# Queueing the low-word step of a float64 weight slice on ScalarE directly behind the high-word step

## The chip, the cores and the metric

The kernel runs on one core of one Trainium2 chip. The metric is the device time of one execution in microseconds (us), taken as the median of several executions. Engines are named as in the profile: PE is TensorE's matmul, PEld its weight load, DVE is VectorE, ACT is ScalarE, POOL is GpSimd, SP is SyncE, which here issues nearly all transfers. "L204" is line 204 of the kernel before; lines of the changed kernel from 210 on stand one higher.

## The reference

The reference has two parts. The first is a recurrent retention layer over 4 batches, 8 heads, 768 positions and head size 64. The second takes its output as 3072 rows of 512 numbers through a two-layer block with SiLU between:

```python
for t in range(S):
    state = gamma[None, :, None, None] * state + np.einsum('bhd,bhe->bhde', k[:, :, t], v[:, :, t])
    y[:, :, t] = scale * np.einsum('bhd,bhde->bhe', q[:, :, t], state)
...
x = np.ascontiguousarray(attn_out.transpose(0, 2, 1, 3)).reshape(B * S, H * D)
...
h = x @ w_in
g = h * (1.0 / (1.0 + np.exp(-h)))
return (g @ w_out).astype(np.float32)
```

q, k and v are float32. The weights `w_in` (512 by 2048) and `w_out` (2048 by 512) come as float64, because they are float32 arrays multiplied by a float64 scalar. The kernel turns them into float32 on the chip.

## The kernel before

**Tiles.** The sequence is cut into 6 chunks of 128 positions; a chunk and a batch make one of 24 units. The retention layer is done by chunks: transposes of k and q, scores within the chunk, a state carried between chunks, and the output y. A "visit" is the work of one step of this pipeline on PE. The first product multiplies, for each chunk c (512 columns, 4 batches) and each of 16 slices f of `w_in` (128 columns), x by the weights. It takes 12 matmuls: x and w are each split in a high and a low part, 8 matmuls go to an accumulator `ha` and 4 to an accumulator `hb`. There are 96 such products, written g c_f below (g 2_14 is chunk 2, slice 14).

**After a product.** ScalarE copies `ha` out of the accumulator (L692, to a buffer `g`), VectorE subtracts `hb` (L697), ScalarE applies SiLU in place (L702), and SP stores the result to DRAM (L708). The `g` buffers rotate over three places, so the copy of product n+3 needs the store of product n to have ended. The accumulators `ha` and `hb` rotate over three banks, two to a product: `hb` of product n+1 uses the bank of `ha` of product n and waits for its copy L692; `ha` of product n+2 uses the bank of `hb` of product n and waits for L697. The second product runs after all first products, from about 360 us on, and reads the stored results back.

**The weight slices.** There are 32 slices, 16 of `w_in` and 16 of `w_out`. Each is loaded as 128 by 512 pairs of 32-bit words (L185 to L189) into a buffer `wf` with two places. Its conversion to float32 is a chain of small steps: ScalarE takes the absolute value of the high words (L204, to `ca`), VectorE takes their sign (L207), ScalarE turns the low words into a float that carries the rounding (L210; for `w_out` it writes over the low words in `wf`, for `w_in` to `cw`), VectorE clamps (L212), shifts (L216) and adds (L222). A converted slice of `w_out` is stored to DRAM (L287) and read back later. The place in `wf` is free for the next load when L222 has run.

**What sets the order.** PE's order is the order of the source. The first part of the kernel, up to where `written` becomes False, has its order on all engines written out by hand. After that the order of ScalarE, VectorE, POOL and SP comes from a scheduler, which places an instruction where it thinks that it can run. `queue(ins)` takes an instruction out of that freedom: what is issued under it is placed behind `ins` on the engine. `take_w`, which starts a slice's conversion after some products, runs under `queue(after)` with the latest L697 as `after`, and L204 stands in a `queue` of its own. The engines run their instructions in the order placed. In the scheduled part the slices from 4 on are converted, and two slices are loaded ahead.

**On ScalarE between products** there are, besides L692, L702, L204 and L210: the copies of the transposed q and k of a unit (L437), the scaling of gq (L357), the high part of x from y (L585, which stands behind a visit on PE), and, near 315 us and later, the split of the `w_out` slices (L120, L126) and of the first stored results (L747).

Of the kernel before, what the change touches and what calls it, by code (L numbers as in the profile page):

```python
# [13 lines left out]
FP32 = mybir.dt.float32  # L14
# [3 lines left out]
AF = mybir.ActivationFunctionType  # L18
# [15 lines left out]
def kernel(  # L34
# [28 lines left out]
    nc = tc.nc  # L63
# [12 lines left out]
    scale = 1.0 / math.sqrt(D)  # L76
# [24 lines left out]
    def bits(x):  # L101
        return float(np.array(x, np.uint32).view(np.float32))
# [89 lines left out]
    def convert_steps(i, out):  # L192

        t = staged.pop(i)
        if not wide:
            out.append(t)
            return
        words = t.rearrange("p (c w) -> p c w", w=2)
        lo, hi = words[:, :, 0], words[:, :, 1]
        a = conv.tile([128, DM], U32, tag="ca", name=f"ca_{i}")  # L200
        s = conv.tile([128, DM], U32, tag="cs", name=f"cs_{i}")
        r = lo if i >= NF else conv.tile([128, DM], U32, tag="cw", name=f"cw_{i}")
        with queue(evac[0] if evac else None):
            nc.scalar.activation(out=a.bitcast(FP32), in_=hi.bitcast(FP32), func=AF.Abs,  # L204
                                 scale=2.0 ** -3)
        yield
        nc.vector.tensor_scalar(out=s, in0=hi, scalar1=0x80000000, scalar2=None,  # L207
                                op0=ALU.bitwise_and)
        yield
        nc.scalar.activation(out=r.bitcast(FP32), in_=lo, func=AF.Copy, scale=2.0 ** -27,  # L210
                             bias=2.0 ** 25)
        nc.vector.tensor_scalar(out=a.bitcast(FP32), in0=a.bitcast(FP32),  # L212
                                scalar1=bits(872 << 20), scalar2=bits((1127 << 20) - 1),
                                op0=ALU.max, op1=ALU.min)
        yield
        nc.vector.scalar_tensor_tensor(out=s, in0=a, scalar=3, in1=s,  # L216
                                       op0=ALU.logical_shift_left, op1=ALU.bitwise_xor)
        yield
        yield
        yield  # L220
        w = s if i < NF else conv.tile([128, DM], U32, tag="cw", name=f"cw_{i}")
        nc.vector.tensor_tensor(out=w, in0=s, in1=r, op=ALU.add)  # L222
        out.append(w.bitcast(FP32))

    def convert_w(i):

        if patient[0]:
            waiting.append(i + W_AHEAD)
        elif i + W_AHEAD not in staged:
            load_w(i + W_AHEAD)  # L230
        out = []
        steps = convert_steps(i, out)
        for _ in range(6):
            next(steps, None)

        def rounded():
            list(steps)
            return out[0]

        return rounded  # L240

    def early_slice(i):

        out = []
        yield from convert_steps(i, out)
        yield
        steps = split_steps(i, out[0], "wi", scale, w_sb, None)
        next(steps)
        yield from steps
# [4 lines left out]
    def queue(ins):  # L254

        return ExitStack() if written[0] or ins is None else tc.issue_after(ins)
# [69 lines left out]
    for j in range(2):  # L326
        for a in range(HP):
            nc.scalar.activation(out=decay[:, j, a, :], in_=lag[:, :D], func=AF.Exp,
                                 scale=float(lg[2 * a + j]))
# [10 lines left out]
    for h in range(H):  # L340
        nc.scalar.activation(out=gk[:, 0, h : h + 1], in_=pos, func=AF.Exp,
                             scale=float(-lg[h]))
# [740 lines left out]
```

## Time and profile before

| | us |
|---|---|
| three executions | 625.62, 621.43, 625.50 (median 625.5) |
| the profiled execution, time | 627.48 |
| the profiled execution, span from first to last instruction | 625.7 |
| mean granted TensorE clock | 0.992 |
| DVE waiting for L692 before L697, whole span | 54.3 |
| ACT waiting for L697 before L702, whole span | 32.9 |
| ACT waiting for `ha` before L692, whole span | 14.5 |
| L210, 16 slices of `w_out` | 10.6 busy, 665 ns each |
| L204, 32 slices | 21.5 busy, 672 ns each |

The span is longer than the sum of any engine's work, so the table is read by asking which wait ends last at each place. A wait of ScalarE or VectorE costs time only where PE then waits for it. The time of an execution that was not profiled lies up to 6 us below that of the profiled one, and the three differ by 4.2 us among themselves.

### The profile page before, as it was taken

The numbers are of one execution on the slowest core, as the hardware profiler recorded it, in microseconds if no ns is written. First come the engines' busy times: TensorE is split into PE (matmuls) and PEld (weight loads), VectorE is DVE, ScalarE is ACT, GpSimd is POOL, SyncE is SP. The second block draws the span as 40 slices with busy tenths as digits, with TensorE's granted clock in tenths as the row PEclk, the third lists the DMA queues.
The fourth block names the chain that finished last, engine by engine and source line by source line (L and its number), as shares of the span: only waits on it lengthen the run. The fifth ranks groups of instructions, "written<-read, shape, count | busy, mean of one in ns | idle before, by whom it ended". The sixth has DMA issues, their size and how long they took to land.

```text
span 625.7 us, 13466 instructions
## 1 busy us (share of the span) xinstructions
PE 602.2 (96%) x5384; PEld 494.4 (79%) x5384; DVE 393.4 (63%) x667; ACT 332.5 (53%) x633; POOL 27.9 (4%) x85
## 2 busy tenths in 40 slices
PE   5798999999999899989999999999999999999997
PEld 4677788888787688878787888888888888888886
DVE  4788788678686557765499593553635544554631
ACT  7677998678675567767588651312312221412311
POOL 3000000100031111111000000000000000000000
PEclk9899999999999899999999999999999999999999
DMA  9998876586699589999769443342533423342301
GB/s 191 224 222 186 235 205 205 165 247 202 236 193 203 155 247 235 273 249 287 252 229 310 160 128 101 121 149 69 170 99 103 167 83 119 136 134 77 126 1 67
DMA packets 144335, 108.88 MB, mean 174 GB/s; under 512 B 101137, under 2 KB 109585, under 8 KB 144273
## 3 DMA queue, kind: packets, MB, share of 16 engines
q1 hardware_dynamic: 141392, 102.79, 59.6%
q10 hardware_dynamic: 2880, 5.24, 2.3%
q8 instruction: 42, 0.69, 0.5%
q14 instruction: 21, 0.16, 0.1%
HBM read 66.06 MB, written 36.70 MB: 164 GB/s over the span
## 4 chain that ended last, share of the span: by engine, by line
PE 91%; DMA 3%; SPq 2%; issue 1%; ACT 1%; DVE 1%; DVEq 0%; POOL 0%; POOLq 0%; ACTq 0%
PE ha L682 27%; PE o L1023 20%; PE oa L1023 14%; PE hb L682 14%; PE ob L1023 7%; PE y L529 4%; DMA wf<-in_moe_w_out_dram 2%; PE sc L480 2%; PE sc L490 1%; DMA kqv<-in_q_dram 1%; SPq L165 1%; DMA vf<-in_v_dram 1%; PE kp L454 1%; PE qp L454 1%; SPq L430 0%
## 5 line engine op out<-in xcount | busy, mean ns | idle before, releaser
L682 PE MATMUL ha<-xt,wi 128*128 128x512 f32 x768 | 195.8, 397 | 0.4 <-ACT xt L585 0.4
L682 PEld LDWEIGHTS ha<-xt,wi 128*128 128x128 f32 x768 | 143.9, 190 | 32.5 <-DVE g L697 0.7
L1023 PE MATMUL o<-wo,gs 128*128 128x512 f32 x564 | 143.1, 389 | 0.0
L747 ACT ACTIVATE gs<-gr 128x512 fp32r<-128x512 f32 x96 | 53.7, 621 | 134.1 <-issue 131.8
L1023 PEld LDWEIGHTS o<-wo,gs 128*128 128x128 f32 x564 | 105.9, 188 | 21.8
L749 DVE TENSOR_TENSOR gs<-gr,gs 128x512 fp32r<-128x512 f32 x96 | 62.2, 687 | 90.2 <-ACT gs L747 90.2
L1023 PE MATMUL oa<-wo,gs 128*128 128x512 f32 x376 | 115.9, 389 | 0.0
L697 DVE TENSOR_TENSOR g<-g,hb 128x512 f32<-128x512 f32 x96 | 65.8, 685 | 73.7 <-ACT g L692 54.3
L682 PE MATMUL hb<-xt,wi 128*128 128x512 f32 x384 | 104.3, 394 | 6.3 <-ACT g L692 6.3
L682 PEld LDWEIGHTS hb<-xt,wi 128*128 128x128 f32 x384 | 72.5, 190 | 23.0 <-ACT g L692 7.9
L1023 PEld LDWEIGHTS oa<-wo,gs 128*128 128x128 f32 x376 | 70.6, 188 | 14.7
L702 ACT ACTIVATE g<-g 128x512 f32<-128x512 f32 x96 | 60.4, 629 | 33.0 <-DVE g L697 32.9
L1023 PE MATMUL ob<-wo,gs 128*128 128x512 f32 x188 | 73.7, 392 | 0.0
L692 ACT ACTIVATE g<-ha 128x512 f32<-128x512 f32 x96 | 56.9, 592 | 16.6 <-PE ha L682 14.5
L750 DVE SCALAR_TENSOR_TENSOR gs<-gs 128x512 fp32r<-128x512 f32 x96 | 62.2, 686 | 0.0
L1023 PEld LDWEIGHTS ob<-wo,gs 128*128 128x128 f32 x188 | 35.3, 188 | 8.7 <-DVE o L1041 1.6
L498 DVE TENSOR_TENSOR am<-sc,decay 128x512 f32<-128x512 f32 x24 | 16.6, 690 | 12.8 <-PE sc L490 12.8
L204 ACT ACTIVATE ca<-wf 128x512 f32<-128x512 f32 x32 | 21.5, 672 | 5.0 <-DVE cs L216 2.6
L210 ACT ACTIVATE wf<-wf 128x512 f32<-128x512 uint32 x16 | 10.6, 665 | 25.2 <-DMA wf<-in_moe_w_out_dram 25.2
L1040 ACT ACTIVATE o<-o 128x512 f32<-128x512 f32 x10 | 6.0, 600 | 33.4 <-PE o L1023 33.0
L216 DVE SCALAR_TENSOR_TENSOR cs<-ca,cs 128x512 uint32<-128x512 uint32 x32 | 22.1, 692 | 0.9
L529 PE MATMUL y<-qt,mid 64*64 64x64 f32 x384 | 20.0, 222 | 2.1 <-issue 1.5
(105 smaller groups left out, 564.4 us busy)
## 6 DMA issues: line engine op xcount, KB each, us to landing
gd<-g SPq DMA_DIRECT2D x96, 256.0 KB, 3.4
gr<-gd SPq DMA_DIRECT2D x96, 256.0 KB, 2.7
wf<-in_moe_w_out_dram SPq DMA_DIRECT2D x16, 512.0 KB, 5.0
out_dram<-o ACTq DMA_DIRECT2D x20, 256.0 KB, 2.1
wf<-in_moe_w_in_dram SPq DMA_DIRECT2D x16, 256.0 KB, 4.0
wf<-in_moe_w_in_dram SPq DMA_DIRECT2D x32, 128.0 KB, 3.8
kf<-in_k_dram SPq DMA_DIRECT2D x16, 256.0 KB, 4.1
qf<-in_q_dram SPq DMA_DIRECT2D x16, 256.0 KB, 4.3
```

Source lines behind the costliest of these rows:

```text
L204: nc.scalar.activation(out=a.bitcast(FP32), in_=hi.bitcast(FP32), func=AF.Abs, scale=2.0 ** -3)
L216: nc.vector.scalar_tensor_tensor(out=s, in0=a, scalar=3, in1=s, op0=ALU.logical_shift_left, op1=ALU.bitwise_xor)
L498: mask = nc.vector.tensor_tensor(out=am[n], in0=sc, in1=decay, op=ALU.mult).ins
L529: i = nc.tensor.matmul(yp[ts(e, D), o, a, :], lhsT=lhsT, rhs=rhs, start=(e, o) not in started, stop=True, skip_group_check=True).ins
L682: nc.tensor.matmul(hb if i == 2 else ha, lhsT=w_sb[f][:, i, ts(kk, 128)], rhs=xt[c][:, i, kk, :], start=kk == 0 and i != 1, stop=kk == KIN ...
L692: copied[:] = [nc.scalar.activation(out=hs, in_=ha, func=AF.Copy, scale=ONE_E).ins]
L697: taken_out[:] = [nc.vector.tensor_tensor(out=hs, in0=hs, in1=hb, op=ALU.subtract).ins]
L702: nc.scalar.activation(out=hs, in_=hs, func=AF.Silu)
L747: nc.scalar.activation(out=t[:, 0, :], in_=g, func=AF.Copy, scale=HALF)
L749: nc.vector.tensor_tensor(out=t[:, 1, :], in0=g, in1=high, op=ALU.subtract)
L750: nc.vector.scalar_tensor_tensor(out=t[:, 2, :], in0=t[:, 1, :].bitcast(FP32), scalar=-1.0 / EPS, in1=high, op0=ALU.mult, op1=ALU.add)
L1023: nc.tensor.matmul(o, lhsT=g, rhs=wo[f][:, i, :], start=f == 0 and i != 1, stop=f == NF - 1 and i != 0)
```

## The change

The instruction that L204 issues is kept as `top`, and the instruction of L210 is issued under `queue(top)`. In the part that is ordered by hand `queue` has no effect. Nothing is computed differently and no instruction is added.

```diff
         with queue(evac[0] if evac else None):
-            nc.scalar.activation(out=a.bitcast(FP32), in_=hi.bitcast(FP32), func=AF.Abs,
-                                 scale=2.0 ** -3)
+            top = nc.scalar.activation(out=a.bitcast(FP32), in_=hi.bitcast(FP32), func=AF.Abs,
+                                       scale=2.0 ** -3).ins
         yield
         nc.vector.tensor_scalar(out=s, in0=hi, scalar1=0x80000000, scalar2=None,
                                 op0=ALU.bitwise_and)
         yield
-        nc.scalar.activation(out=r.bitcast(FP32), in_=lo, func=AF.Copy, scale=2.0 ** -27,
-                             bias=2.0 ** 25)
+        with queue(top):
+            nc.scalar.activation(out=r.bitcast(FP32), in_=lo, func=AF.Copy, scale=2.0 ** -27,
+                                 bias=2.0 ** 25)
```

## The prediction

> **What bounds the kernel now.** I read the page's first part, then the table of stretches, the list of waits, and the timeline around the longest wait. The first part says that PE is the engine to follow:
>
> ```profile
> span 625.7 us, 13466 instructions
> PE 602.2 (96%) x5384; PEld 494.4 (79%) x5384; DVE 393.4 (63%) x667; ACT 332.5 (53%) x633; POOL 27.9 (4%) x85
> ```
>
> PE idles 23.5 us in all. Nothing but those idle times, and what follows from them, can be won by moving a ScalarE instruction. Where they lie is in the stretches (start:end, length, busy time of PE, PEld, DVE, ACT, POOL, granted clock, DMA share, GB/s):
>
> ```profile
> 162.00:175.00 13.00, 12.82 (x175) 10.33 (x174) 9.40 (x16) 8.33 (x16) 1.64 (x3) 1.00 0.68 227
> 196.00:210.00 14.00, 9.60 (x117) 7.61 (x108) 5.41 (x10) 7.14 (x11) 0.09 (x1) 0.88 0.89 171
> 210.00:264.00 54.00, 54.00 (x696) 44.78 (x695) 37.43 (x65) 35.34 (x57) 8.45 (x12) 1.00 0.91 234
> 264.00:281.00 17.00, 15.27 (x169) 12.32 (x169) 10.71 (x20) 10.98 (x17) 2.11 (x3) 1.00 1.08 261
> ```
>
> The reader is to see that one stretch of 14 us holds 4.4 us of idle PE and a granted clock of 0.88, that 264 to 281 holds 1.7 us more, and that 210 to 264 is full. The list of waits names who keeps PE there:
>
> ```profile
> ACT wf L210 <- DMA wf<-in_moe_w_out_dram: 25.2, 12, 6.4
> PE hb L682 <- ACT g L692: 6.3, 3, 4.4
> ACT ca L204 <- DMA wf<-in_moe_w_out_dram: 2.2, 2, 1.3
> ACT g L692 <- DMA gd<-g: 1.0, 3, 0.6
> ```
>
> L210 sits idle for 25.2 us because its slice has not landed; only 6.3 us of that reaches PE, at three places. The longest, from the timeline (start, duration; others between left out):
>
> ```profile
> 196.82 0.66 ACT L204 ACTIVATE ca<-wf 128x512 f32<-128x512 f32 x1
> ...
> 197.67 0.63 ACT L702 ACTIVATE g<-g 128x512 f32<-128x512 f32 x1 [0.19 <-DVE g L697]
> ...
> 198.21 0.58 ACT L585 ACTIVATE xt<-y 128x512 fp32r<-128x512 f32 x1
> ...
> 200.04 0.38 SPq L189 DMA_DIRECT2D wf<-in_moe_w_out_dram  x1
> 200.04 1.97 PE L682 MATMUL ha<-xt,wi 128*128 128x512 f32 x8
> ...
> 205.23 0.65 ACT L210 ACTIVATE wf<-wf 128x512 f32<-128x512 uint32 x1 [6.44 <-DMA wf<-in_moe_w_out_dram]
> 205.79 0.58 ACT L692 ACTIVATE g<-ha 128x512 f32<-128x512 f32 x1
> ...
> 206.42 2.02 PE L682 MATMUL hb<-xt,wi 128*128 128x512 f32 x4 [4.40 <-ACT g L692]
> ```
>
> The L210 of slice 20 is placed before its load is issued (200.04). ScalarE stands until 205.23, the copy L692 of g 2_14 stands behind it, and `hb` of g 2_15 waits for that copy's bank. When it starts, its four matmuls take 2.02 us where an undisturbed set takes 1.07.
>
> **The change, part by part.** The instruction order of the changed program differs from the order before on ScalarE alone; DVE, POOL, SP and PE have the same lists. On ScalarE 15 instructions L210 move: those of slice 6 and of fourteen of the sixteen `w_out` slices (21 and 25 already stand directly behind their L204). They go from a place in front of an L692, L702 or L585 to one behind L204 of the same slice, some 3 to 28 us later; at slices 18 and 29 an L702 (and an L692) still stand between the two. A few steps of L120, L126 and L747 change places with neighbours. No DMA moves in its queue, and nothing is added: the 15 times 0.67 us of work stays.
>
> *Removed: the waits of L210.* At the L204 of the same slice the load has landed already. Slice 20 lands at 205.2 and its L204 runs at 214.32; slice 26 lands at 273.9, its L204 runs at 282.74; slice 22 at 232.4 and 241.29; slice 18 at 163.0 and 165.57. L204 itself waits for a load at two slices only (21 and 25, 2.2 us in sum, the third row above), and PE waits at neither.
>
> What the three PE waits cost is read from the distance between products. Undisturbed, one `ha` starts 2.72 us after the other (147.03 and 149.75).
> - First place (A): slice 19's L210 holds g 1_14's copy until 170.31. `hb` starts at 170.94 instead of 170.60 and the visit behind it at 172.09 instead of 171.60 (1.00 behind `hb`, as from 178.78 to 179.78): 0.5 us.
> - Second (B): `ha` of g 2_15 starts at 200.04, that of g 3_1 at 211.76, two products later. Two times 2.72 is 5.44, so 11.72 - 5.44 = 6.3 us are lost: 4.4 of wait and 1.9 of slow matmuls.
> - Third (C): slice 26's L210 waits until 273.99, g 4_2's copy runs at 275.03; from `ha` at 271.96 to the next at 276.70 it is 4.74, so 2.0 us.
>
> Together 8.8 us. That is the most the change can bring by this route.
>
> About the 1.9: the granted clock of 0.88 over 14 us is 1.7 us of lost clock, and the slow matmuls give 1.9. The Trainium skill, page "TensorE: Matmul & The Clock Gate", Part 1, has the clock fall to half after an idle window of about 3.4 us, and those windows run free of the kernel. By that rule B would be priced at 4.4 + 1.7 = 6.1 instead of 6.3, the gain below would be 0.2 smaller, and an execution in which the windows lie otherwise would not pay it.
>
> *What is late next in B.* With L210 gone, ScalarE runs L692 of g 2_14 when `ha` is ready, near 199.2, then the copies L437 of q (landed 197.3) and k. The k transpose's landing is not in the trace; it is issued over 195.72 to 199.33, and the one like it at 271.95, held up 3.17 us, lands 5.3 after its start, so I take 201.5. Then L437 ends near 202.8 (1.3), L702 near 203.3 and L692 of g 2_15 runs at 203.4, in time for the `hb` that could start at 204.6. The next copy, g 3_0, needs the buffer of g 2_13, whose store is issued at 201.51 and lands 7.2 us later, at 208.7, behind 1.3 MB of other transfers issued from 199.4 on. SP's list is unchanged and none of those transfers waits for PE, so I keep 208.7. `hb` starts 0.63 after the copy's start (205.79 to 206.42), so at 209.3 where 207.3 was possible: 2.0 us, and 0.15 of restart as in C (1.89 late at `hb`, 2.02 at the next `ha`). So 2.2 us of B come back as a wait for a store that today is hidden under the longer one. Bounds: nothing, if that store lands as fast as the one at 199.38 (2.9 us); 2.2 if as in the trace. I take 2.2, because it is the same transfer behind the same queue. An idle time of 2 us did not lower the clock in C (granted 1.00), so no slow matmuls are added.
>
> In A, the transfers of `yr` at 165.99 and 166.59 (landing 171.1) now end the wait in front of L585; the copy g 1_14 runs in front of it, so PE is free: 0.5 stays won. In C the buffer that g 4_2 needs (store at 264.05, 3.1 us) is free, and k's copy is far: 2.0 stays won.
>
> *Added: L210 beside L204.* One L210 costs 0.56 us of ScalarE's time there (270.51 minus 269.93 is 0.58, 230.75 minus 230.20 is 0.55). Mostly it delays L702 by 0.4, because L702 waits for L697 anyway (0.19 idle behind L204 alone). The cover is the 2.72 us of a product, of which L692, L204, L210, L702 and L585 take 0.48 + 0.56 + 0.56 + 0.52 + 0.48 = 2.6, and behind a visit PE gives 2 us more. So nothing; if the cover goes, 0.4 per slice. Slice 6 is taken out before 82.55 and put in at 91.65; ScalarE has no idle time between 83.9 and 92.2, so the 0.57 that it gains at the first place is what it spends at the second: zero. Slices 30 and 31 near 328 and 337: two products there start 0.2 and 0.3 us late already, by a buffer wait; between -0.3 and +0.5, I take zero. L222 of a slice runs 5 us or more behind L204 in nearly all cases, so VectorE does not wait for the later L210, `wf` comes free as before, and the loads keep their times.
>
> A rule speaks against setting two functions side by side. The trace has two ACT_TABLE_LOADs of 1.28 us, both at the start, and at 230.20 a L210 follows a L204 0.59 after its start, with no load between. The Trainium skill, "ScalarE: Activation LUTs", section "Table sets: the hidden batching unit", tells authors to batch by table set; if Abs and Copy lay in different sets, 15 moved steps with one load each would add 15 x 1.28 = 19.2 us. The rows give zero, and I take zero.
>
> *Sum.* A 0.5 + B (6.3 - 2.2) + C 2.0 = 6.6 us. The profiled execution, 627.48 us (span 625.7 and 1.8 around it), would become 620.9. It is 2.0 above the median; on the median 625.5 it makes 618.9.
>
> **The rivals.**
> - *The store is no wait.* It lands in time for g 3_0, and the whole 8.8 is won: 616.7. For: the store before it took 2.9. Against: 7.2 in this trace.
> - *Less was lost to begin with.* One of three executions took 621.43. If 4 us of B (a shorter held-up transpose, no half clock) are absent in many executions, only 2.5 to 4.5 us remain: 621 to 623. For: the spread of 4.2. Against: two of three and the profiled one are long.
> - *Slower: the stores fall behind.* Each L702 behind L204 and L210 is up to 0.56 later, its store too, and L692 three products on waits for that store; L692 waited for a store three times already (1.0 us). If that slack is gone at all 14 moved `w_out` places, PE loses 14 x 0.56 = 7.8, and with B's wait grown by the same store to its old 6.3, A and C win 2.5: 5.3 slower, 630.8. It decides only if stores take over 2 x 2.72 = 5.4 us in most products; the median to landing is 3.4.
> - *The change does nothing:* L204 now waits for the load in L210's place. Then 625.5. The landing times above speak against it at all but two slices.
>
> **How the numbers follow.** A change under 1% (619.2 to 631.8) can't be told from none here. Forecast 618.9 with 617.7 to 620.5 around it: 0.50. Store no wait, 615.5 to 617.7: 0.20. Less lost, 620.5 to 623.5: 0.18. Nothing, 0.05. Slower, 0.07. The forecast lies near the 1% line: 0.32 of its 0.50 fall below it, and with the 0.20 faster has 0.52; slower than 631.8 gets 0.04, since the slower case itself lies at 630.8; the rest, 0.44, is within 1%. The range 615.5 to 622.5 leaves out the slower and the idle case and a part of the third: about 2 in 10.
>
> **What would show it.** Right: L210 no longer in the list of waits for the load; ScalarE's L210 running right behind L204; around 200 us a PE wait of about 2 us on L692 and L692 waiting for `gd<-g`; a granted clock of 1.00 there; no PE wait near 274. Wrong: L204 inheriting waits of several us; L692 waiting for stores at many products; PE waiting for L437's k transpose; an `hb` wait over 3.4 us with the clock down again.

## The result, and the profile after

| | us |
|---|---|
| the changed kernel, median of 10 executions | 618.01 (617.11 to 619.40) |
| the kernel before beside it, median of 10 | 624.08 (621.43 to 625.62) |
| ratio, 95% interval | 0.9909, 0.9887 to 0.9931 |
| profiled execution of the changed kernel | 618.27, span 616.5, clock 0.994 |

The change is worth 6.1 us by the two medians, 0.9% by the ratio. The ratios in this document are taken over the executions in the chip's fast state alone and are not the quotient of the two medians beside them. Lines of the changed kernel from 210 on stand one higher: L211 is the low-word step, L693 the copy of `ha`, L698 the subtraction, L703 SiLU, L709 the store. The first part of the page:

```profile
span 616.5 us, 13474 instructions
PE 602.1 (98%) x5384; PEld 496.7 (81%) x5384; DVE 392.4 (64%) x667; ACT 332.4 (54%) x633; POOL 27.7 (4%) x85
```

PE is busy for as long (602.1 us against 602.2) in a span that is 9.2 us shorter. The same four stretches as before (start:end, length, busy time of PE, PEld, DVE, ACT, POOL, granted clock, DMA share, GB/s) are now full, and the clock in the second is whole:

```profile
162.00:175.00 13.00, 13.00 (x178) 10.76 (x177) 10.50 (x18) 8.48 (x16) 2.11 (x3) 1.00 0.75 244
196.00:210.00 14.00, 14.00 (x221) 11.69 (x214) 9.55 (x18) 10.71 (x18) 1.22 (x3) 1.00 0.82 213
210.00:264.00 54.00, 54.00 (x680) 44.72 (x679) 38.12 (x66) 37.00 (x59) 9.33 (x13) 1.00 0.97 251
264.00:281.00 17.00, 17.00 (x179) 14.09 (x178) 10.43 (x17) 10.99 (x17) 2.11 (x3) 1.00 1.04 259
```

In the list of waits between 80 and 360 us there is no row of L211 left, and none of PE waiting for L693. What is left of the two DMA rows of ScalarE, with PE's only other wait:

```profile
ACT g L693 <- DMA gd<-g: 2.9, 5, 0.8
...
ACT ca L204 <- DMA wf<-in_moe_w_out_dram: 1.5, 1, 1.5
...
PE y L530 <- POOL token L385: 0.3, 1, 0.3
```

L204 waits at one slice, not for all; L693 waits for a store five times, 0.8 us at the longest. The place that was B, in the timeline (start, duration):

```profile
196.27 0.39 SPq L189 DMA_DIRECT2D wf<-in_moe_w_out_dram  x1
...
198.77 0.60 ACT L693 ACTIVATE g<-ha 128x512 f32<-128x512 f32 x1 [0.35 <-ACT xt L586]
199.26 1.35 ACT L438 COPY qt<-qw 128x1024 uint16<-128x1024 uint16 x1
199.43 1.98 PE L683 MATMUL ha<-xt,wi 128*128 128x512 f32 x8
...
201.24 1.07 PE L683 MATMUL hb<-xt,wi 128*128 128x512 f32 x4
...
204.21 0.60 ACT L693 ACTIVATE g<-ha 128x512 f32<-128x512 f32 x1
...
207.42 0.67 ACT L204 ACTIVATE ca<-wf 128x512 f32<-128x512 f32 x1
207.99 0.68 ACT L211 ACTIVATE wf<-wf 128x512 f32<-128x512 uint32 x1
```

L693 of g 2_14 runs at 198.77 with no L211 ahead of it, `hb` follows with no wait and at full speed (1.07), and the low-word step of slice 20 stands behind its L204 at 207.99, when the slice has long landed. The copy of g 3_0 at 204.21 waits for no store: the 2.2 us that the prediction let come back are not in this execution.

### The profile page after: what moved, and what is told of

Same layout as the page of the kernel before. It is cut to its first block, busy times and chain, and to the rows that moved or that the text cites. A ratio compares the mean times of both kernels' runs of the same rounds, so it can differ in the third digit from the quotient of the medians.

```text
span 616.5 us, 13474 instructions
## 1 busy us (share of the span) xinstructions
PE 602.1 (98%) x5384; PEld 496.7 (81%) x5384; DVE 392.4 (64%) x667; ACT 332.4 (54%) x633; POOL 27.7 (4%) x85
## 4 chain that ended last, share of the span: by engine, by line
PE 97%; DVE 1%; issue 1%; DMA 1%; DVEq 0%; POOL 0%; POOLq 0%
PE ha L683 29%; PE o L1024 21%; PE hb L683 14%; PE oa L1024 14%; PE ob L1024 7%; PE y L530 5%; PE sc L481 2%; PE sc L491 2%; PE kp L455 1%; PE qp L455 1%; DMA kqv<-in_k_dram 1%; PE o L1032 0%; DVE am L499 0%; PE oa L1032 0%; PE kp L462 0%
## 5 line engine op out<-in xcount | busy, mean ns | idle before, releaser
L698 DVE TENSOR_TENSOR g<-g,hb 128x512 f32<-128x512 f32 x96 | 65.7, 684 | 65.5 <-ACT g L693 39.7
L683 PE MATMUL hb<-xt,wi 128*128 128x512 f32 x384 | 102.9, 390 | 0.0
L703 ACT ACTIVATE g<-g 128x512 f32<-128x512 f32 x96 | 60.3, 628 | 36.7 <-DVE g L698 36.4
L693 ACT ACTIVATE g<-ha 128x512 f32<-128x512 f32 x96 | 56.9, 592 | 29.1 <-PE ha L683 20.9
L204 ACT ACTIVATE ca<-wf 128x512 f32<-128x512 f32 x32 | 21.4, 670 | 4.1 <-DVE cs L217 2.5
L530 PE MATMUL y<-qt,mid 64*64 64x64 f32 x384 | 20.3, 225 | 1.2 <-POOL token L385 1.2
L592 DVE SCALAR_TENSOR_TENSOR xt<-xt 128x512 fp32r<-128x512 f32 x28 | 19.1, 689 | 0.6
```

Of the source, the lines that this page charges most:

```text
L204: top = nc.scalar.activation(out=a.bitcast(FP32), in_=hi.bitcast(FP32), func=AF.Abs, scale=2.0 ** -3).ins
L530: i = nc.tensor.matmul(yp[ts(e, D), o, a, :], lhsT=lhsT, rhs=rhs, start=(e, o) not in started, stop=True, skip_group_check=True).ins
L592: nc.vector.scalar_tensor_tensor(out=x[2], in0=x[1].bitcast(FP32), scalar=-1.0 / EPS, in1=x[0].bitcast(FP32), op0=ALU.mult, op1=ALU.add)
L683: nc.tensor.matmul(hb if i == 2 else ha, lhsT=w_sb[f][:, i, ts(kk, 128)], rhs=xt[c][:, i, kk, :], start=kk == 0 and i != 1, stop=kk == KIN ...
L693: copied[:] = [nc.scalar.activation(out=hs, in_=ha, func=AF.Copy, scale=ONE_E).ins]
L698: taken_out[:] = [nc.vector.tensor_tensor(out=hs, in0=hs, in1=hb, op=ALU.subtract).ins]
```

## The experiments

Two groups of kernels were timed in several rounds, each group beside the kernel before, and single profiled executions were added. To compare profiles, each product's start is read as the start of its first `ha` matmul. The stretch between two starts less the same stretch of the profiled changed kernel gives the loss at A, B, C and behind B, where the store of g 2_13 was forecast to be late. B is the two products from `ha` of g 2_15 on, "behind B" is the next one, A and C are one product each. The time of an execution is then 517.6 us, plus the start of the fifteenth product (near 100 us), plus the losses: 517.6 + 100.8 + 9.1 gives 627.5 for the profile of before (627.48). All of it in us; "SP held" is the duration of the k transpose on SP ahead of slice 20's load:

| profile | time | 15th product | A | B | behind B | C | all losses | SP held |
|---|---|---|---|---|---|---|---|---|
| before | 627.48 | 100.79 | 0.48 | 6.28 | 0 | 2.02 | 9.09 | 3.61 |
| before_again | 627.50 | 101.19 | 0.27 | 5.81 | 0 | 2.09 | 8.65 | 3.14 |
| before_look | 626.04 | 99.29 | 0.01 | 7.93 | 0.02 | 0.98 | 9.11 | 3.86 |
| before_look2 | 629.03 | 100.40 | 0 | 7.41 | 0.02 | 2.86 | 11.01 | 3.65 |
| before_look3 | 623.28 | 99.21 | 0.02 | 5.88 | 0 | 0.69 | 6.43 | 3.08 |
| after | 618.27 | 100.65 | 0 | 0 | 0 | 0 | 0 | 1.29 |
| after_again | 616.87 | 98.27 | 0 | 0 | 0.63 | 0 | 0.96 | 3.44 |
| after_look2 | 617.57 | 99.56 | 0 | 0 | 0 | 0 | 0.41 | 2.09 |
| after_look3 | 622.90 | 102.66 | 0 | 0 | 2.33 | 0 | 2.53 | 3.83 |
| only_19_20_26 | 620.55 | 102.21 | 0 | 0 | 0 | 0 | 0.67 | 1.87 |
| only_20 | 619.12 | 99.12 | 0.19 | 0 | 0.69 | 1.24 | 2.38 | 3.51 |
| all_but_three | 624.22 | 101.82 | 0 | 4.03 | 0 | 0.68 | 4.75 | 1.72 |
| all_but_20 | 623.61 | 102.33 | 0 | 3.80 | 0 | 0 | 3.64 | 2.29 |
| double_high | 622.36 | 103.50 | 0 | 0 | 0 | 0 | 1.25 | 1.75 |

Losses at other places are in the sum alone; in before_look2 0.92 of them is slow matmuls right behind C. The two groups had different medians of before, 626.62 and 625.57, and the expectations in microseconds were written for the 625.5 of the first three executions, so the ratios are compared.

**The kernel before again (before_again).** No edit.

> The kernel before, unchanged, for a second profile. Theory (three waits of L210 reach PE, the second of a size that hangs on when slice 20's load is issued): the three places are there again, near 170, 202 and 274 us, with about 0.5 and 2 us at the first and third; the second is between 2 and 6.5 us, and the span is as much shorter as the second is smaller. Rival (the spread of 4 us of this kernel lies elsewhere, at the start or the end): the second place loses 6.3 us again whatever the span. Time 621 to 626.

Median of 12 executions 625.9 against 626.62 of 29; ratio 0.9982, 0.9946 to 1.0018. So a difference of 0.2% comes out of nothing here, and an interval is some ±0.35% wide. Its profile loses at the same three places.

**The three slices alone (only_19_20_26).** The instruction is queued behind L204 for three slices, and placed freely for the others:

```diff
-        with queue(top):
+        with queue(top if i in (19, 20, 26) else None):
```

> Only the three slices whose L210 reached PE (19, 20, 26) have their low-word step behind the high-word step. Theory: the whole gain is there, 617.5 to 619. Rival (ScalarE gains everywhere from the 25 us of waits that go, and the gain comes from many places): less than half of the gain, 621 or more.

Median 619.85, ratio 0.989 (0.9852 to 0.9928): the whole gain with 3 of the 15 moved instructions, as far as six executions can tell. One thing was not foreseen. From its timeline, slice 27:

```profile
280.57 0.67 ACT L211 ACTIVATE wf<-wf 128x512 f32<-128x512 uint32 x1 [3.46 <-DMA wf<-in_moe_w_out_dram]
...
282.25 1.20 PE L683 MATMUL hb<-xt,wi 128*128 128x512 f32 x4 [0.53 <-ACT g L693]
```

Slice 27's step, still free, waits 3.46 us, and 0.53 of that reaches PE, 0.82 in starts. In the profile of before it reached PE nowhere. Which free low-word step gets in front of a copy depends on when the loads are issued in that execution.

**Slice 20 alone (only_20).**

```diff
-        with queue(top):
+        with queue(top if i == 20 else None):
```

> Only slice 20's low-word step is moved. Theory: the second place alone is won, the 0.5 and 2.0 us of the first and third stay: 2.5 above the changed kernel, 620 to 621. Rival (all of the gain is the second place): 618. Rival (many places): 623 or more.

Median 623.2, ratio 0.9926 (0.9892 to 0.9961); its profiled execution took 619.12, the shortest of the twelve. From its timeline, at B and at C:

```profile
205.26 0.60 ACT L693 ACTIVATE g<-ha 128x512 f32<-128x512 f32 x1 [2.05 <-DMA gd<-g]
205.91 1.20 PE L683 MATMUL hb<-xt,wi 128*128 128x512 f32 x4 [0.41 <-ACT g L693]
...
267.75 1.20 PE L683 MATMUL hb<-xt,wi 128*128 128x512 f32 x4 [0.95 <-ACT g L693]
```

B is gone. The copy of g 3_0 waits 2.05 us for the store, as forecast in kind, but only 0.41 of it is idle PE; the rest was slack. C is still there (1.24), and slice 26 was not moved. The ratio is that of the theory (620 to 621 of 625.5 is 0.991 to 0.993); the median lies at the second rival's 623, but beside a kernel before of 626.62.

**All but the three (all_but_three).**

```diff
-        with queue(top):
+        with queue(top if i not in (19, 20, 26) else None):
```

> All slices except 19, 20 and 26 have their low-word step moved. Theory: as the kernel before, all three places are there again, 623.5 to 625 (0.4 may be won near 330 us). Rival (many places): 619 to 621.

Median 624.12, ratio 0.9966 (0.9936 to 0.9997). The profile keeps B and C in smaller size, 4.03 and 0.68, and has no A, though slice 19 was not moved. The list of waits and the timeline at B:

```profile
ACT wf L211 <- DMA wf<-in_moe_w_out_dram: 8.1, 3, 4.3
PE hb L683 <- ACT g L693: 2.6, 2, 2.2
```

```profile
200.59 1.98 PE L683 MATMUL ha<-xt,wi 128*128 128x512 f32 x8
...
204.78 2.07 PE L683 MATMUL hb<-xt,wi 128*128 128x512 f32 x4 [2.22 <-ACT g L693]
```

A is missing although slice 19's L211 waits 1.96 us here; it is missing in three of the five profiles of before too (0.02 or less), so this profile doesn't show what A hangs on. Three of the L211 waits are left, and slice 20's alone makes 2.2 of the 2.6 us of idle PE. The ratio's interval leaves out 1: either the other twelve slices are worth something (2 us by its middle), or it is noise, since the unchanged kernel came to 0.9982.

**All but slice 20 (all_but_20).**

```diff
-        with queue(top):
+        with queue(top if i != 20 else None):
```

> All slices except 20 have their low-word step moved. Theory: A and C are won, B stays with 4 to 6.3 us: ratio to before 0.993 to 0.997. Rival (B is not where the time went): as the changed kernel, 0.990.

Median 624.23, ratio 0.9989 (0.9959 to 1.0019): with slice 20 left out the gain is gone as far as this can be measured. That is above the 0.993 to 0.997 expected: the 2.5 us of A and C don't show in the executions, though the interval has room for 2.6, and in the profile C is indeed empty. Its list of waits has one row of L211:

```profile
ACT wf L211 <- DMA wf<-in_moe_w_out_dram: 4.6, 1, 4.6
```

Against the complete change in the same group (0.9901) slice 20 is worth 0.0088 of 625.6, 5.5 us; by the two medians (624.23 and 619.87) it is 4.4, and by only_20 4.6 (ratio) or 3.4 (medians). The profile says 3.8, at a late start (102.33). So slice 20 makes 3.4 to 5.5 us of some 6.

**The changed kernel again (after_again).** No edit.

> The changed kernel, unchanged, for a second profile on this chip. Theory: no wait of PE on the copy L693 between 80 and 360 us over 1 us; ratio to before 0.988 to 0.992; if the store of g 2_13 lands late, a wait of L693 for gd of up to 2 us near 205 us with under 1 us lost on PE, otherwise none. Rival (the store takes the place of the load in every execution): 2 us lost on PE near 205.

Median 619.87 against 625.57, ratio 0.9901 (0.9868 to 0.9933), the first result again. The profile has a bit of the store:

```profile
ACT g L693 <- DMA gd<-g: 8.3, 9, 2.1
...
PE hb L683 <- ACT g L693: 0.6, 2, 0.3
```

Nine waits for stores, 8.3 us, of which 0.6 reach PE.

**The high-word step twice (double_high).** To see whether the added L211 beside L204 is hidden, L204 is issued a second time for each `w_out` slice, 16 times 0.56 us of ScalarE, 9 us:

```diff
+            if i >= NF:
+                with queue(top):
+                    top = nc.scalar.activation(out=a.bitcast(FP32), in_=hi.bitcast(FP32),
+                                               func=AF.Abs, scale=2.0 ** -3).ins
```

> The changed kernel with the high-word step of the 16 slices of w_out run twice (the second writes the same values again): 16 x 0.56 = 9 us more of ScalarE time at the same places, the rest in nearly the same order. It prices the cover of the moved step. Theory (ScalarE's time beside the high-word step is hidden): at most 1 us slower than the changed kernel, ratio to before 0.988 to 0.993. Rival (the budget of 2.72 us a product is full and each step costs what it takes): 4 to 9 us slower, ratio 0.996 to 1.005.

Median 620.84, ratio 0.9929 (0.99 to 0.9958), against 0.9901 (0.9868 to 0.9933) of the changed kernel in the same group: 0.3% by the middle of two intervals that overlap. The stretch that holds nearly all the doubled steps, first of double_high, then of after_again:

```profile
162.00:360.00 198.00, 197.17 (x2159) 162.12 (x2158) 145.43 (x244) 150.59 (x252) 20.49 (x30) 1.00 0.86 240
```

```profile
162.00:360.00 198.00, 197.13 (x2161) 162.46 (x2160) 144.13 (x245) 140.41 (x233) 20.40 (x30) 1.00 0.88 237
```

ScalarE (fourth sum) has 10.2 us more and PE (first) is as full as without. One place loses 0.79 us. So another 0.56 us beside L211 at each slice costs a small part of its 9 us: 1.0 by the two medians, 1.25 in this profile, some 1.8 by the two ratios, where at most 1 was expected and 4 to 9 if nothing hid it.

**Single profiled executions** of the kernel before (before_look, before_look2, before_look3) and of the changed one (after_look2, after_look3), to see what varies.

> The kernel before, one more profile. If its time is near 621, theory: the second place loses 2 to 3 us only, because the load of slice 20 is issued nearer to its L210 (below 198.5 us), and the clock keeps to 1.00. If near 625 or more: the second place loses 4 to 6.3 us.

> The kernel before, one more profile, to see what a shorter execution lacks. Theory: its time is the start (product 14 begins between 98 and 103 us whatever the kernel) plus what B loses; B loses 3.8 to 4.1 where PE's wait stays under 3 us and no half clock follows in full, 6 to 8 where the wait is 4 us or more. A time of 621 to 623 goes with a B of about 4 or an early start. Rival: B is always 6 to 8 and all of the spread is the start.

> As the one before it: B of 4 or of 6 to 8, A 0 to 0.5, C 1 to 2; the rest of the distance between products as in the changed kernel to within 0.6 us.

> The changed kernel, one more profile. Theory: A, B and C under 0.1, a store wait that costs PE 0 to 0.7 near 205 us; the time follows the start of product 14. Rival: a wait of 2 us or more at one of the places in some executions.

> The changed kernel unchanged, one more profiled execution. By the profiles so far the body of the changed kernel loses 0 to 1.0 us between product starts and the body before 6.4 to 11.0, while the medians differ by 6.1 and 5.7. If the profiles are right, this one loses at most 1.5 us in the body, and its time is set by where the 14th product starts: 517.8 us plus that start, within 1.5. If the medians are right and the profiles of the changed kernel so far were lucky ones, the body loses 2 to 4 us, at places to be read from its waits.

The five profiles of before lose 6.4 to 11.0 us, B always the largest part (5.8 to 7.9), C between 0.7 and 2.9. The light B of 2 to 4 us that three of these expectations allowed for did not turn up, and the 7.93 of before_look is more than the 4 to 6.3 expected there. Nor is the spread all in the start, as the rival had it: before_look2 and before_look3 are 5.75 us apart, and 1.2 of it is the start. after_look2 loses 0.4. after_look3 took 622.90 and loses 2.53, the second case of its expectation: the profiles before it had been light ones. Nearly all of it lies at one known place. Its timeline there:

```profile
197.13 3.83 SPq L431 DMA_TRANSPOSE kw<-kp  x1
...
201.43 1.98 PE L683 MATMUL ha<-xt,wi 128*128 128x512 f32 x8
201.67 0.38 SPq L189 DMA_DIRECT2D wf<-in_moe_w_out_dram  x1
...
203.13 9.43 SPq L709 DMA_DIRECT2D gd<-g  x4
...
206.41 0.63 ACT L703 ACTIVATE g<-g 128x512 f32<-128x512 f32 x1 [0.75 <-DVE g L698]
206.87 1.98 PE L683 MATMUL ha<-xt,wi 128*128 128x512 f32 x8
210.23 0.60 ACT L693 ACTIVATE g<-ha 128x512 f32<-128x512 f32 x1 [3.19 <-DMA gd<-g]
...
210.88 1.20 PE L683 MATMUL hb<-xt,wi 128*128 128x512 f32 x4 [2.04 <-ACT g L693]
```

This is the forecast wait for the store, nearly to the digit. SP is held at the k transpose for 3.83 us, so slice 20's load leaves 0.24 behind `ha` of g 2_15 (0.00 in the profile of before). The store of g 2_13 leaves at 203.13 and lands at 210.13, 7.0 us later. The copy of g 3_0 waits 3.19 for it and PE 2.04; the forecast was 7.2 to landing and 2.0 of idle PE. That the digits agree is luck, as the other three profiles show.

## Why the prediction was right, point by point

**What is lost, and where: right.** With L211 behind L204 all three places are empty in the four profiles of the changed kernel, and a change of three slices has the whole gain. Slice 20 makes 3.4 to 5.5 us of it. Slices 19 and 26 make the step from 0.9926 to 0.989, 2.3 us where A and C were put at 2.5; both differences carry intervals of some ±2 us, and all_but_20 doesn't show this step.

**A, 0.5: too high.** It is 0 to 0.48 in five profiles of before (mean 0.16), and the prediction had the one with the most.

**B, 6.3, and C, 2.0: right in size.** The five profiles give means of 6.7 and 1.7. C has its half clock in one profile only.

**The slow matmuls, 1.9: right for this trace, not for each.** They are a part of B in each of the five: the clock fell to half there in all of them, and nowhere from the fifteenth product to 600 us in the changed kernel's four. Their price differs: B less PE's wait is 1.7 to 1.9 in three profiles and 3.0 in the two where the half clock lasts twice as long (before_look, before_look2). Nor does every execution pay it: of the 70 executions of before timed in the two groups, three (621.54, 621.63 and 623.10) have a mean clock of 0.999 or more, which leaves at most 1.9 us at half clock, less than the 3.41 that the shortest fall lasts. The prediction's reason for adding no slow matmuls to the store's wait, that 2 us of idle PE did not lower the clock at C, holds for that trace alone: 1.88 us lowered it in before_look2 and 2.22 in all_but_three. In after_look3 2.04 us did not.

**What comes back, 2.2: right as one case, wrong as the case.** This is the step that failed: "SP's list is unchanged and none of those transfers waits for PE, so I keep 208.7". 208.7 is 8.7 us behind the start of `ha` of g 2_15. The store lands 4.4 us behind it in the first profile of the changed kernel, 7.0 in after_again, and 8.7 only in after_look3. So 0, 0.63, 0 and 2.33 us come back, 0.74 on average. The list is the same, but its times are not: the k transpose holds SP 1.29, 3.44, 2.09 and 3.83 us in these four, in the same order as the loss, and the other three profiles with slice 20 moved agree: 1.75 and 1.87 with no loss, 3.51 with 0.69. In the five profiles of before it was 3.1 to 3.9, and I had one of these. Forecast and rival ("the store is no wait") are two ends of one quantity that differs between executions. A kernel with a fourth `g` buffer, which would take the store out of it, was not tried.

**Added at no cost: right.** No profile of the changed kernel has the ACT_TABLE_LOADs that a change of function would have to show: there are two of 1.28 us, as before. The Trainium skill, "ScalarE: Activation LUTs", section "Table sets: the hidden batching unit", lists abs and copy among the cheap functions that every set contains, which agrees with this count; the batching that it asks for concerns other pairs. Double_high shows the cover: 9 us more, 1.25 lost in its profile.

**Profile to median: nearly right.** Four profiles of the changed kernel have a mean of 618.9 and five of before one of 626.7: 7.8 us apart, where the sum said 6.6. The medians are 6.1 apart in the first result and 5.7 in the second (6.2 by ratio, 4.2 to 8.3). The smaller return of the store makes the profiles' difference larger than forecast. That the medians' difference is smaller I can't explain from nine profiles. The first profile of before, 627.48, was longer than all ten executions timed in the first result (621.43 to 625.62), and the start of the fifteenth product alone moves by 5.2 us in the table. So it is luck in part that 6.6 came near 6.1: the return of the store was put 1.5 too high, and the medians show 1.7 less than the profiles.

**The rivals.** The store as no wait was right in two profiles of four. "Less was lost to begin with" exists: before_look3 took 623.28 with 6.4 lost, but no profile came down to the 2.5 to 4.5 that the rival needed; four of the first ten executions of before took 621.4 to 621.8, shorter than any profiled one, and what these lost is not known. The stores falling behind: L693 waits up to nine times, 8.3 us in all in after_again, but PE takes 0.6 of it; the slack of 0.56 per product was never gone at all places. That the change does nothing fell with L204's waits, 1.5 us at one slice.

**Open.** Why SP is held for 3.1 to 3.9 us in every profile of before and often less in the changed kernel is not settled. all_but_three and all_but_20 have short ones (1.72, 2.29) and a smaller B, as if the other moved slices let SP go earlier; but all_but_20's median does not show a smaller B. The table's profiles show where to look: in the four in which the k transpose is issued 5.2 us ahead of `ha` of g 2_15 it holds SP for 1.3 to 1.9 us, in the other ten, 3.6 to 4.5 us ahead, for 2.1 to 3.9.

## What to carry to other kernels

In this kernel, and it may be so in others, ScalarE runs its instructions in the order placed. There an instruction that waits for a transfer should stand behind a step that needs the same transfer anyway; placed ahead of it by a scheduler, it makes everything behind it wait, and that costs only where the bottleneck engine needs one of those things (here 6.3 us of 25.2, plus what the clock takes). When such a wait goes, look for the next late thing at that place, and give it a distribution: its size came from transfer times that one trace shows once, and four traces showed at 0 to 2.3 us. One slice carried most of the gain, but which slice gets in the way differs between executions, as slice 27 showed; that speaks for moving all of them, though no run here shows more gain from all than from three.

## What the hardware showed that was not expected

**The clock falls after a window that is only partly idle.** The granted clock changes on a grid of 3.41 us that is different in each execution. In all_but_three PE waits just 2.22 us, of which 2.02 lie in the window that ends at 204.58, 59% of it, and the clock is at half from there to 208.00: the `hb` behind it takes 2.07 instead of 1.07. In before_look2 a wait of 1.88 us at C is 55% of its window and the clock falls at 276.31. In all_but_20 a longer wait, 2.80 us, is spread over two windows, 29% and 53% of them, and the clock stays whole. The stretches 196 to 214 of all_but_20, and 196 to 214 and 264 to 284 of before_look2 (the granted clock is the third number from the end):

```profile
196.00:214.00 18.00, 14.80 (x234) 11.57 (x236) 10.20 (x19) 11.62 (x21) 0.09 (x1) 1.00 0.81 184
```

```profile
196.00:214.00 18.00, 13.62 (x73) 10.71 (x64) 7.50 (x14) 8.14 (x13) 0.00 (x0) 0.81 0.71 155
264.00:284.00 20.00, 18.12 (x176) 14.46 (x174) 11.79 (x20) 12.39 (x18) 2.12 (x3) 0.91 1.02 260
```

The Trainium skill, "TensorE: Matmul & The Clock Gate", Part 1, has the fall come after an idle window of about 3.4 us on a free-running grid. The grid agrees (3.41). If the window is taken to be idle throughout, the rule does not hold: beside these products of 128 by 512, 55% was enough and 53% was not. It is no rule for all work on PE: in the first 30 us, where PE runs matmuls of 64 by 64, a window 37% idle (all_but_three, 20.3 to 23.7) was followed by a fall and one 47% idle (before_look3, 22.9 to 26.3) was not. So the idle share alone does not decide.

**It comes back after a busy window, not after a fixed time.** In before_look2 the clock falls at 204.63 and PE starts again at 205.52, so 26% of the next window is idle; the half clock lasts two windows, 6.83 us. In before_look3 it falls at 203.83 and PE starts at 204.13, 9% idle, and it lasts one, 3.41. How full a window must be is not settled: in before_again the half clock of 22.57 lasts three windows, 10.24 us, of which the second is only 8% idle, with small matmuls.

**The time to the fifteenth product varies by 5 us whatever the kernel, and goes with the clock.** after_look3 has 13.7 us of half clock within its first 60 us and reaches that product at 102.66; after_again has none and reaches it at 98.27. Of the 14 profiles the five with no half clock there (before_look, before_look3, after_again, after_look2, only_20) reach it at 98.3 to 99.6, the other nine at 100.4 to 103.5. Which of the two causes the other is not shown.
